# An S5 scan gated by an MLP, on one core: a bias through a broadcast load, B turned by DMA, C loaded late, a warm-up burst and a searched order

## The chip, the cores and the metric

The kernel runs on one core of a Trainium2 chip. A core has five engines that run side by side, each through its own list of instructions in order: TensorE (PE, matrix products into psum), VectorE (DVE), ScalarE (ACT, functions by table), GpSimd (POOL) and SyncE (SP), which here only issues DMAs. They wait for each other through semaphores. Tensors come from HBM into SBUF (128 partitions) by DMA; psum has eight banks. The metric is the device time of one execution in microseconds; of several runs the median is taken.

## The reference

The input x has 2048 rows of D = 448. It is normalised (`xn`), and two branches work on it: a complex diagonal recurrence with P = 448 states (branch A), and an MLP with F = 1792 behind a second LayerNorm (branch B). The result is x + A * silu(B).

```python
def _A_ref(x, ...):                     # x is xn
    Lam, Bmat, Cmat = Lambda_re + 1j*Lambda_im, B_re + 1j*B_im, C_re + 1j*C_im
    Lam_bar = jnp.exp(jnp.exp(log_dt) * Lam)
    B_bar = ((Lam_bar - 1.0) / Lam)[:, None] * Bmat
    Bu = jnp.einsum("bld,pd->blp", x + 0j, B_bar)
    for t in range(L):
        h = Lam_bar[None, :] * h + Bu[:, t, :]
    y = 2.0 * jnp.einsum("blp,dp->bld", hseq, Cmat).real + x * Dskip

def _B_ref(x, w1, b1, w2, b2):
    h = _gelu(jnp.einsum("bsd,df->bsf", _layernorm(x), w1) + b1)
    return jnp.einsum("bsf,fd->bsd", h, w2) + b2

s = _A_ref(xn, ...);  g = _silu(_B_ref(xn, ...));  return x + s * g
```

Weights and x are bf16, as is the output.

## The kernel before

**Tiling.** The rows go in four groups `g` of 512; a group has two blocks `b` of 256 rows, and a block has even and odd rows (`par`). The scan is taken over pairs of rows, so it has 256 steps a group (NK). The matmul stages of a group are:

- `xt`: LayerNorm's results `xn` (branch A) and `xn2` (branch B, its row of ones carries b1) are turned into `xnT` and `xn2T`. For `xn2` of group 0 this is done on PE with `ident` (L390) and copied out by ACT and DVE, for all others by DMA on SP (`dma_start_transpose`, L73).
- `bu(g, i)`: xn times the combined B matrix `BT` into psum bank 4 (L558; 14 matmuls of 256 columns for i = 0, 1, 2, and 7 for i = 3). ACT evacuates it into `u_sb` (L562 to L566), which frees the bank for the next.
- `ssm(g)`: rotation by the tables `WT`, scans on DVE (L583), and rotation back into `h_sb`.
- `mm1(g, j)`: xn2 times w1 (L623, 8 matmuls of 512 columns for each of seven j) into bank pairs 0/1 and 2/3; ACT's gelu (L630) writes `gT[:, g % 2]`.
- `mm2(g, b, par)`: gT times w2 (L637, 14 matmuls) into bank 5 or 6, and one more matmul (L639) that adds b2 by `onesblk` (its first row ones) and `b2blk` (its first row b2). Then ACT's tanh(x/2) (L641), and g = (tanh + 1) * psum on DVE (L642); the halves are folded into other factors.
- `ym(g, b, par)`: h times `CZ` or `CQ`, and the skip through `M0` or `Do`, into bank 7 (L651 to L659); DVE multiplies by g (L663), adds x (L664) and SP stores.

**Preparation.** `parameters` brings the four vectors onto partitions by nine small matmuls (L408 to L412), DVE copies them out (`cp`, L415), and some forty small operations on POOL, with ACT's exp and sin and one reciprocal on DVE (L449), make the coefficients. `tables` makes WT (DVE L479 to L489, ACT L485 to L491). `lb(m)` makes the B matrix that takes two steps at once (`combine`, seven pairs on DVE), and `bt_pe(m)` turns it: seven PE transposes (L520) into bank 6 or 7, one evacuation by DVE (L526) or ACT (L524). C is loaded in twelve pieces into `Cn`, which lies in the half of gT that groups 1 and 3 use (keys GA), over a zero fill by POOL (L284); `ct_dma` turns it with four DMAs into `Cr`, and `cq` combines it into CQ and CZ, fourteen pairs of an ACT scale (L501) and a DVE multiply-add (L504). `m0` multiplies B by CQ (L547, L549).

**What sets the order.** No order is written out by hand. Each operation is a Task with an engine, a planned duration `dur` and latency `lat`, keys that it reads and writes, and a priority. `order()` simulates a list schedule: of all ready tasks it takes the one with the earliest possible start, and at equal starts the lowest `prio`. `emit()` writes the instructions in that order, engine by engine, with the waits that the keys ask for. So a change of a duration or a priority in the code moves instructions everywhere. Each DMA is a task of the engine that issues it and has its own semaphore. Priorities come from the stage: P gives ln -9, bu -8, mm1 0, mm2 5, ym 6, and 10 more for each group; group 0 and the preparation have values of about -100 to -57.

w2 is loaded by two DMAs of POOL, everything else by SP but for the four vectors (ACT).

Of the kernel before, what the change touches and what calls it, by code (L numbers as in the profile page):

```python
# [15 lines left out]
class Task:
# [5 lines left out]
                 "deps", "succ", "start", "end", "name")  # L22

    def __init__(self, eng, ins, reads, writes, dur, lat, prio, sem, nbytes, name):
# [4 lines left out]
        self.start = self.end = None  # L29


class Plan:
# [25 lines left out]
    def add(self, eng, ins, reads=(), writes=(), dur=0.2, lat=0.1, prio=0.0, sem=None, nbytes=0, name=""):  # L58
        if callable(ins):
            ins = [ins]  # L60
        t = Task(eng, ins, reads, writes, dur, lat, prio, sem or eng, nbytes, name)
# [4 lines left out]
    def dma(self, eng, out_ap, in_ap, reads=(), writes=(), prio=0.0, nbytes=0, transpose=False, name="dma"):
# [105 lines left out]
def bass_recurrent_scan__ssm_conv_s5__mixer_channel_mlp__prompt_kernel(  # L172
# [15 lines left out]
    PK = 3  # L188

    kb = Plan(nc)  # L190
    with ExitStack() as es:
# [70 lines left out]
        with nc.Block():  # L262
# [21 lines left out]
            pool(lambda e: e.memset(Cn, 0.0), [], ["Cnp"], 2.0, S0 + 1)  # L284
# [475 lines left out]
```

## Time and profile before

| | us |
|---|---|
| median of three runs | 178.13 |
| lowest and highest of them | 178.11, 179.58 |
| the profiled execution, its own time | 177.91 |
| its span, first to last instruction | 175.9 |

The page of the profile gives, for one execution, the busy time of each engine, the same in 40 slices of 4.4 us, the DMA queues, the chain of work that ended last, and groups of instructions by line with their mean length in ns and the idle time ahead of them. PE's matmuls are pipelined and their ends are modelled: a group's mean length holds the way through the array, and the spacing of matmuls in a stream is read from the chain, where a run of matmuls stands with its length. PEld is the loading of PE's weights, which overlaps the matmuls. An engine's idle time matters only where the chain passes through it.

| part | busy us | of the span |
|---|---|---|
| PE | 157.7 | 90% |
| DVE | 116.2 | 66% |
| ACT | 91.0 | 52% |
| POOL | 35.7 | 20% |

### The profile page before, as it was taken

The numbers are of one execution on the slowest core, as the hardware profiler recorded it, in microseconds if no ns is written. First come the engines' busy times: TensorE is split into PE (matmuls) and PEld (weight loads), VectorE is DVE, ScalarE is ACT, GpSimd is POOL, SyncE is SP. The second block draws the span as 40 slices with busy tenths as digits, with TensorE's granted clock in tenths as the row PEclk, the third lists the DMA queues.
The fourth block names the chain that finished last, engine by engine and source line by source line (L and its number), as shares of the span: only waits on it lengthen the run. The fifth ranks groups of instructions, "written<-read, shape, count | busy, mean of one in ns | idle before, by whom it ended". The sixth has DMA issues, their size and how long they took to land.

```text
span 175.9 us, 2656 instructions
## 1 busy us (share of the span) xinstructions
PE 157.7 (90%) x942; PEld 88.1 (50%) x942; DVE 116.2 (66%) x262; ACT 91.0 (52%) x137; POOL 35.7 (20%) x98
## 2 busy tenths in 40 slices
PE   0149999789989999999999999999999999999971
PEld 0143445666656544545566654656555454455430
DVE  4798997669998997998751499611798722013342
ACT  3047659897879874757182244972326424411200
POOL 8979993000013500320000002120000000000000
PEclk9999999999999999999999999999999999999999
DMA  5999999619300000013953402100000101000011
GB/s 131 332 287 286 310 266 151 123 25 131 72 2 0 4 0 0 0 52 86 130 117 68 104 4 52 52 0 0 4 0 0 52 0 52 4 0 0 0 52 54
DMA packets 25272, 13.21 MB, mean 75 GB/s; under 512 B 19878, under 2 KB 24907, under 8 KB 25260
## 3 DMA queue, kind: packets, MB, share of 16 engines
q1 hardware_dynamic: 24836, 11.45, 30.1%
q0 software_dynamic: 416, 1.61, 2.9%
q8 instruction: 7, 0.11, 0.2%
q14 instruction: 5, 0.04, 0.1%
q10 hardware_dynamic: 8, 0.00, 0.0%
HBM read 6.89 MB, written 1.84 MB: 50 GB/s over the span
## 4 chain that ended last, share of the span: by engine, by line
PE 81%; ACT 8%; POOL 4%; DVE 3%; issue 1%; ACTq 0%; POOLq 0%
PE psum L623 27%; PE psum L637 23%; PE psum L651 12%; PE psum L558 10%; PE psum L655 3%; PE psum L547 2%; POOL gT L284 2%; PE psum L639 2%; DVE t L663 1%; PE psum L390 1%; ACT gT L630 1%; ACT BT L524 1%; PE psum L659 1%; ACT L630 1%; ACT L641 1%
## 5 line engine op out<-in xcount | busy, mean ns | idle before, releaser
L623 PE MATMUL psum<-xn2T,w_sb 128*128 128x512 bf16 x224 | 51.8, 386 | 1.0 <-DVE xn2T L396 1.0
L637 PE MATMUL psum<-w_sb,gT 128*128 128x448 bf16 x224 | 45.0, 352 | 0.8 <-ACT BT L524 0.5
L630 ACT ACTIVATE gT<-psum 128x1024 bf16<-128x1024 f32 x28 | 28.6, 1022 | 25.0 <-PE psum L623 24.8
L623 PEld LDWEIGHTS psum<-xn2T,w_sb 128*128 128x128 bf16 x224 | 21.9, 99 | 26.4 <-issue 1.9
L637 PEld LDWEIGHTS psum<-w_sb,gT 128*128 128x128 bf16 x224 | 21.7, 98 | 20.1 <-issue 0.7
L642 DVE SCALAR_TENSOR_TENSOR g_sb<-th,psum 128x448 bf16<-128x448 f32 x16 | 9.9, 617 | 30.0 <-ACT th L641 30.0
L558 PE MATMUL psum<-xnT,BT 128*128 128x256 bf16 x196 | 24.0, 273 | 1.3 <-ACT u_sb L562 1.3
L558 PEld LDWEIGHTS psum<-xnT,BT 128*128 128x128 bf16 x196 | 18.8, 98 | 5.8 <-PE psum L549 1.1
L641 ACT ACTIVATE th<-psum 128x448 f32<-128x448 f32 x16 | 8.6, 541 | 23.2 <-PE psum L639 23.1
L663 DVE TENSOR_TENSOR t<-psum,g_sb 128x448 bf16<-128x448 f32 x16 | 9.9, 622 | 11.9 <-PE psum L659 6.5
L597 POOL TENSOR_TENSOR cwk<-s_f,ang 128x3 f32<-128x3 f32 x3 | 1.6, 526 | 64.1 <-DVE s_f L583 64.1
L583 DVE TENSOR_TENSOR_SCAN s_f<-cw,cur,v_sb 128x256 f32<-128x256 f32 x21 | 14.5, 736 | 0.0
L651 PE MATMUL psum<-CZ,h_sb 128*128 128x448 bf16 x56 | 11.9, 353 | 0.7 <-DVE t L663 0.7
L651 PE MATMUL psum<-CQ,h_sb 128*128 128x448 bf16 x56 | 11.9, 353 | 0.7 <-DVE t L663 0.7
L562 ACT ACTIVATE u_sb<-psum 128x512 bf16<-128x512 f32 x12 | 7.1, 593 | 7.1 <-PE psum L558 7.1
L345 DVE BATCH_NORM_STATS2 lnst<-x_all 128x6 f32<-128x448 bf16 x16 | 9.6, 616 | 0.9 <-DMA x_all<-in_A_x_dram 0.9
L501 ACT ACTIVATE tmp<-Cr,cw 128x448 f32<-128x448 bf16 x14 | 9.2, 665 | 1.3 <-DVE CQ L504 1.2
L377 DVE TENSOR_SCALAR xn_sb<-x_all,lnw 128x448 bf16<-128x448 bf16 x24 | 8.7, 404 | 1.7 <-DMA xnT<-xn_sb 1.6
L651 PEld LDWEIGHTS psum<-CQ,h_sb 128*128 128x128 bf16 x56 | 5.4, 98 | 6.1 <-DVE t L663 1.2
L651 PEld LDWEIGHTS psum<-CZ,h_sb 128*128 128x128 bf16 x56 | 5.4, 98 | 5.9 <-DVE t L663 0.9
L587 ACT ACTIVATE s_b<-s_f 128x1536 bf16<-128x1536 f32 x4 | 5.9, 1478 | 2.9 <-DVE s_f L583 2.9
L655 PE MATMUL psum<-M,xnT 128*128 128x448 bf16 x32 | 7.4, 353 | 0.0
(130 smaller groups left out, 183.1 us busy)
## 6 DMA issues: line engine op xcount, KB each, us to landing
w_sb<-in_B_w_dram POOLq DMA_DIRECT2D x2, 784.0 KB, 9.4
out_dram<-o_sb SPq DMA_DIRECT2D x7, 224.0 KB, 1.9
w_sb<-in_B_w_dram SPq DMA_DIRECT2D x2, 672.0 KB, 6.5
x_all<-in_A_x_dram SPq DMA_DIRECT2D x3, 448.0 KB, 6.5
x_all<-in_A_x_dram SPq DMA_DIRECT2D x2, 224.0 KB, 2.6
Bn<-in_A_B_re_dram SPq DMA_DIRECT2D x1, 336.0 KB, 8.5
Bn<-in_A_B_im_dram SPq DMA_DIRECT2D x1, 336.0 KB, 7.7
gT<-in_A_C_re_dram SPq DMA_DIRECT2D x1, 288.0 KB, 7.3
```

The costliest lines, as they stand in the source:

```text
L345: dve([lambda e, b=b, par=par, q=q: e.bn_stats(lnst[:, q, :], x_all[:, 2 * g + b, par, :])], [f"x{2 * g + b}"], [f"st{q}"], 0.6, prio)
L501: act(lambda e: e.activation(tmp[:, k, :], b, ACT.Copy, scale=cb), rd, [f"tmp{k}"], 0.66, prio)
L558: fns = [lambda e, r=r, m=m, d=d: e.matmul(psum[:, 4, r * NK:(r + 1) * NK], BT[:, m, d, :], xnT[:, gx, d, :], start=(d == 0), stop=(d == 6 ...
L583: dve(lambda e, i=i, ri=ri, init=init: e.tensor_tensor_scan(s_f[:, i, ri, :], col(R2, i).to_broadcast([128, NK]), v_sb[:, i, ri, :], init, ...
L623: fns = [lambda e, k=k, d=d: e.matmul(psum[:, b0 + k, :], w1_sb[:, d, (2 * j + k) * 128:(2 * j + k + 1) * 128], rhs[:, d, :, :], start=(d ...
L630: act(lambda e: e.activation(gT[:, gb, 2 * j:2 * j + 2, :], psum[:, b0:b0 + 2, :], ACT.Gelu_apprx_tanh), [f"ps{b0}", f"ps{b0 + 1}"] + (WK ...
L637: fns = [lambda e, fi=fi: e.matmul(psum[:, bk, 0:D], gT[:, gb, fi, q * 128:(q + 1) * 128], w2_sb[:, fi, :], start=(fi == 0), stop=False) f ...
L641: act(lambda e: e.activation(th[:, fb, :], psum[:, bk, 0:D], ACT.Tanh, scale=0.5), [f"ps{bk}"] + (WK + WKP if g == 0 else []), [f"th{fb}"] ...
L642: dve(lambda e: e.scalar_tensor_tensor(out=g_sb[:, gs, :], in0=th[:, fb, :], scalar=1.0, in1=psum[:, bk, 0:D], op0=ALU.add, op1=ALU.mult), ...
L651: fns = [lambda e, k=k: e.matmul(psum[:, 7, 0:D], h_sb[:, hb, k, k0:k0 + 128], cm[:, k, :], start=(k == 0), stop=False) for k in range(7)]
L655: fns += [lambda e, d=d: e.matmul(psum[:, 7, 0:D], xnT[:, gx, d, xs], M0[:, d, :], start=False, stop=(d == 3)) for d in range(4)]
L663: dve(lambda e: e.tensor_tensor(t3[:, fb, :], psum[:, 7, 0:D], g_sb[:, gs, :], ALU.mult), ["ps7", f"g{gs}"], [f"t3{fb}"], 0.62, prio - 75)
```

## The change

1. **b2.** `onesblk`, `b2blk` and their fills go, and so does the sixteenth matmul of each mm2. b2 is loaded by one DMA into all 128 partitions (`b2bc`, each partition reads the same 896 B). DVE adds it: `o2` = psum + b2bc, in F32 in SBUF. tanh and g read o2, so the bank of mm2 is free after the add.
2. **B.** `bt_pe` goes. `bt(m)` is one DMA transpose of a whole tile on SP, 128 x 896, seven of them, each behind its `lb(m)`.
3. **C.** Cn lies in four blocks of 112 rows rather than 128, so nothing has to be filled with zeros (POOL's fill goes). It comes in five loads rather than twelve, with priority -40, where the loads ahead of it have the fixed ones below; the columns of Cr are renumbered.
4. **Loads.** Loads of x (first two blocks), w1, b1, B, w2, b2 and blocks 2 and 3 of x have priorities near -1e6 (PINNED = -1e5), which set them in the order of the code; w2 moves from POOL to SP.
5. **Warm-up.** 40 matmuls of `ident` with itself into bank 3 are put first on PE: 28, and 12 that read `cp`, at that place in the code before anything has written it.
6. **LayerNorm.** The ten steps of `ln_scale` are one task (`chain=True`) that nothing is put between.
7. **POOL and DVE.** De and Do, eight scalings of `ident`, move from POOL to DVE.
8. **Order.** Of the tasks of the engine whose task could start first, all that could start within 0.13 us (SLACK) compete, and the lowest priority wins. `search` tries six mixes of the priorities with the length of the path behind each task, then 2500 random changes, and keeps what makes the planned total smallest; pinned tasks are left alone. Some planned durations are new.
9. **Memory.** `o_sb` is now a view of `tmp`.

The core of the diff:

```diff
+PINNED = -1e5
+SLACK = 0.13
...
-        dur = nbytes / 105e3 if transpose else 0.45
+        if transpose:
+            dur = 1.4
...
+            first = min(ready, key=lambda t: (starts[t], t.prio, t.idx))
+            limit = starts[first] + SLACK
+            t = min((t for t in ready if t.eng == first.eng and starts[t] <= limit), key=lambda t: (t.prio, t.idx))
...
+    def search(self, rounds, seed=1):
+        tail = {}
+        for t in reversed(self.tasks):
+            tail[t] = t.dur + max([tail[s] + (t.lat if s.eng != t.eng else 0.03) for s in t.succ], default=0)
...
+        for alpha in (0.0, 0.1, 0.3, 1.0, 3.0, 1000.0):
+            trial([p - alpha * tail[t] if p > PINNED else p for t, p in zip(self.tasks, given)])
...
+        o_sb = tmp.bitcast(BF)
+        b2bc = SB("b2bc", [128, D])
+        o2 = SB("o2", [128, 2, D], F32)
...
-            pool(lambda e: e.memset(Cn, 0.0), [], ["Cnp"], 2.0, S0 + 1)
...
             for q in range(2):
-                ld("pool", w2_sb[:, q * 7:q * 7 + 7, :],
+                ld("sp", w2_sb[:, q * 7:q * 7 + 7, :],
...
+            ld("sp", b2bc[:], dram_ap(B_b2, 0, [[0, 128], [1, D]]), ["b2bc"], 114688, S1 + 7)
+            ldx(2, 2, S1 + 7)
...
+                    ld("sp", Cn[0:112, :, o:o + n], dram_ap(cm, a, [[D, 112], [112 * D, 4], [1, n]]), [f"Cn{o}"], 448 * n * 2, -40, dur=1.2)
...
-            def bt_pe(m, bank, how, prio):
-                pe([lambda e, d=d: e.transpose(psh[:, bank, d * 128:(d + 1) * 128], Bn[:, m, d * 128:(d + 1) * 128],
-                                               ident[:, :]) for d in range(7)], rd, [f"ps{bank}"], 0.5, prio)
...
+            def bt(m, prio):
+                rd = [f"Bn{m // 3}"] if m < 6 else ["Bn60", "Bn61"]
+                kb.dma("sp", BT[:, m, :, :], Bn[:, m, :], reads=rd + [f"LB{m}"], writes=[f"BT{m}"], prio=prio, nbytes=229376, transpose=True)
...
-                fns.append(lambda e: e.matmul(psum[:, bk, 0:D], onesblk[:, :], b2blk[:, :], start=False, stop=True))
...
+                dve(lambda e: e.tensor_tensor(o2[:, fb, :], psum[:, bk, 0:D], b2bc[:], ALU.add), [f"ps{bk}", "b2bc"], [f"oo{fb}"], 0.62, prio - 76)
+                act(lambda e: e.activation(th[:, fb, :], o2[:, fb, :], ACT.Tanh, scale=0.5), [f"oo{fb}"] + (WK + WKP if g == 0 else []), [f"th{fb}"], 0.58, prio - 75)
...
+            for k, (n, rd) in enumerate(((28, []), (12, ["cp"]))):
+                pe([lambda e: e.matmul(psum[:, 3, 0:128], ident[:, :], ident[:, :], start=True, stop=True) for _ in range(n)],
+                   ["ident"] + rd, ["ps3"], n * (0.115, 0.06)[k], 2 * PINNED)
...
-            kb.emit()
+            kb.emit(2500)
```

How the order moves at three places. **First, PE behind mm1 of group 0**, before (L623 is mm1, L520 the transposes of B, L637 and L639 mm2, L558 bu):

```order
L623 MATMUL psum<-xn2T,w_sb 128x512 x56
L520 MATMUL psum<-ident,Bn 128x128 x14
L637 MATMUL psum<-w_sb,gT 128x448 x14
L639 MATMUL psum<-b2blk,onesblk 128x448
L520 MATMUL psum<-ident,Bn 128x128 x14
L558 MATMUL psum<-xnT,BT 128x256 x14
L520 MATMUL psum<-ident,Bn 128x128 x14
L558 MATMUL psum<-xnT,BT 128x256 x14
```

and now (L659 is mm1, L594 bu, L673 mm2):

```order
L659 MATMUL psum<-xn2T,w_sb 128x512 x56
L594 MATMUL psum<-xnT,BT 128x256 x14
L673 MATMUL psum<-w_sb,gT 128x448 x14
L594 MATMUL psum<-xnT,BT 128x256 x14
L673 MATMUL psum<-w_sb,gT 128x448 x14
L594 MATMUL psum<-xnT,BT 128x256 x14
L673 MATMUL psum<-w_sb,gT 128x448 x14
L594 MATMUL psum<-xnT,BT 128x256 x7
L659 MATMUL psum<-xn2T,w_sb 128x512 x8
L594 MATMUL psum<-xnT,BT 128x256 x14
L659 MATMUL psum<-xn2T,w_sb 128x512 x8
L594 MATMUL psum<-xnT,BT 128x256 x14
```

Behind mm1 came transposes and mm2, with bu third; bu is now the first work behind it, and needs xnT and two tiles of BT there. The queue of SP that brings them, before, from the last loads of C on:

```order
L74 DMA gT<-in_A_C_im_dram 64x64
L74 DMA b2blk<-in_B_b_dram 1x448
L74 DMA x_all<-in_A_x_dram 128x2x896 x2
L73 DMA_TRANSPOSE xnT<-xn_sb 128x7x128 x2
L73 DMA_TRANSPOSE Cr<-gT 128x8x128 x3
L73 DMA_TRANSPOSE Cr<-gT 128x8x64
L73 DMA_TRANSPOSE xn2T<-xn_sb 128x8x128 x2
L73 DMA_TRANSPOSE xnT<-xn_sb 128x7x128 x2
```

and now, from w2 on:

```order
L82 DMA w_sb<-in_B_w_dram 128x7x448 x2
L82 DMA b2bc<-in_B_b_dram 128x448
L82 DMA x_all<-in_A_x_dram 128x2x896
L82 DMA gT<-in_A_C_re_dram 112x4x64
L82 DMA gT<-in_A_C_re_dram 112x4x448
L81 DMA_TRANSPOSE xnT<-xn_sb 128x7x128
L81 DMA_TRANSPOSE BT<-Bn 128x7x128 x2
L81 DMA_TRANSPOSE xnT<-xn_sb 128x7x128
L81 DMA_TRANSPOSE BT<-Bn 128x7x128 x3
L82 DMA gT<-in_A_C_im_dram 112x4x384
L81 DMA_TRANSPOSE BT<-Bn 128x7x128 x2
L82 DMA gT<-in_A_C_im_dram 112x4x64 x2
```

The seven BT stand among the loads, the first two between the xnT of group 0; behind these rows come two loads of x, xn2T and xnT of group 1, and then the four Cr, which before stood ahead of xn2T.

**Second, ACT where gelu of group 1 begins** (the first gelu that writes over C). Before, with the waits (s_d37 to s_d40 are the four Cr; L641 is tanh, L562 to L566 the evacuation of bu, L630 gelu, L501 the scale in cq):

```order
L501 ACTIVATE tmp<-Cr,cw 128x448 [waits s_d39,s_d38,s_d37,s_pool,s_d40]
L562 ACTIVATE u_sb<-psum 128x512 [waits s_pe]
L501 ACTIVATE tmp<-Cr,cw 128x448
L501 ACTIVATE tmp<-Cr,cw 128x448 [waits s_dve,s_act]
L641 ACTIVATE th<-psum 128x448 [waits s_pe]
```

and now (L677 is tanh, L598 to L602 the evacuation of bu, L666 gelu, L544 the scale):

```order
L677 ACTIVATE th<-o 128x448 [waits s_dve,s_act]
L598 ACTIVATE u_sb<-psum 128x512 [waits s_pe]
L666 ACT_TABLE_LOAD [waits s_d39,s_d38,s_d37]
L666 ACTIVATE gT<-psum 128x1024 [waits s_d40]
L598 ACTIVATE u_sb<-psum 128x512 [waits s_act,s_pe]
L666 ACTIVATE gT<-psum 128x1024
L544 ACTIVATE tmp<-Cr,cw 128x448 [waits s_pool]
```

The wait for Cr stood at a scale behind the third BT evacuation; it now stands at gelu's table load, with the evacuation of bu(1,1) queued behind it.

**Third, the end of PE.** Before, from the last mm2 on (L651 to L659 are ym):

```order
L637 MATMUL psum<-w_sb,gT 128x448 x14
L639 MATMUL psum<-b2blk,onesblk 128x448
L651 MATMUL psum<-CQ,h_sb 128x448 x7
L658 MATMUL psum<-Do,xnT 128x64
L659 MATMUL psum<-Do,xnT 128x128 x3
L651 MATMUL psum<-CZ,h_sb 128x448 x7
L655 MATMUL psum<-M,xnT 128x448 x4
L651 MATMUL psum<-CQ,h_sb 128x448 x7
L658 MATMUL psum<-Do,xnT 128x64
L659 MATMUL psum<-Do,xnT 128x128 x3
```

and now (L687 to L695 are ym):

```order
L673 MATMUL psum<-w_sb,gT 128x448 x14
L687 MATMUL psum<-CQ,h_sb 128x448 x7
L694 MATMUL psum<-Do,xnT 128x64
L695 MATMUL psum<-Do,xnT 128x128 x3
L673 MATMUL psum<-w_sb,gT 128x448 x14
L687 MATMUL psum<-CZ,h_sb 128x448 x7
L691 MATMUL psum<-M,xnT 128x448 x4
L687 MATMUL psum<-CQ,h_sb 128x448 x7
L694 MATMUL psum<-Do,xnT 128x64
L695 MATMUL psum<-Do,xnT 128x128 x3
```

Three ym stood behind the last mm2; two do now.

227 lines of the change are left out of this document (119 added, 108 removed).

## The prediction

> **What bounds the kernel now.** I read the page first: busy shares, the slices, DMA.
>
> ```profile
> PE 157.7 (90%) x942; PEld 88.1 (50%) x942; DVE 116.2 (66%) x262; ACT 91.0 (52%) x137; POOL 35.7 (20%) x98
> PE   0149999789989999999999999999999999999971
> DMA  5999999619300000013953402100000101000011
> GB/s 131 332 287 286 310 266 151 123 25 131 72 2 0 4 0 0 0 52 86 130 117 68 104 4 52 52 0 0 4 0 0 52 0 52 4 0 0 0 52 54
> ```
>
> A slice is 4.4 us. PE is full from the third slice to the end, but for slices 7 to 9; DMA is full in the first seven slices only. So the time is a start without PE, the PE stream, and an end behind PE. The chain of waits (start us, length us, what) gives the pieces and the pace of each kind of PE work; the waits of PE follow it (total, times, longest).
>
> ```profile
> 1.10 0.27 POOL ident L266
> ...
> 2.19 3.51 POOL gT L284
> ...
> 8.60 0.18 DVE cw L449
> ...
> 10.13 1.90 PE psum L390 x16
> ...
> 12.05 0.70 DVE xn2T L396
> ...
> 13.00 13.54 PE psum L623 x56
> ...
> 28.41 1.28 ACT L485
> ...
> 36.32 0.54 ACT th L641
> ...
> 40.47 0.19 PE psum L639
> 40.66 1.53 PE psum L558 x14
> 42.18 2.65 PE psum L637 x14
> ...
> 45.02 0.78 PE psum L558 x7
> ...
> 60.78 1.73 PE psum L623 x8
> ...
> 166.89 0.64 DVE t L663
> ...
> 169.87 0.64 DVE t L663
> ```
>
> ```profile
> PE psum L408 <- DMA vrows<-in_A_Dskip_dram: 4.9, 1, 4.9
> ...
> PE psum L558 <- ACT u_sb L562: 1.3, 2, 0.8
> PE psum L637 <- ACT BT L524: 0.5, 1, 0.5
> PE psum L520 <- DVE BT L526: 0.4, 1, 0.4
> PE psum L637 <- ACT gT L630: 0.3, 1, 0.3
> ```
>
> The reader sees: PE starts its stream at 13.00, waits 2.5 us in all behind that, and twice more, 0.64 us and some each, at the very end, where ym has one psum bank and DVE must free it. Everything else is PE work. A change gains what it takes out of the PE stream, out of the start, or out of the end, less the new waits it puts into the stream.
>
> **The change part by part.** I write mm1, mm2, bu, ym as the code does; mm2(0,1) is of group 0.
>
> *b2.* Sixteen matmuls of L639 leave PE.
>
> ```profile
> L639 PE MATMUL psum<-b2blk,onesblk 128*128 128x448 bf16 x16 | 5.6, 352 | 0.0
> L642 DVE SCALAR_TENSOR_TENSOR g_sb<-th,psum 128x448 bf16<-128x448 f32 x16 | 9.9, 617 | 30.0 <-ACT th L641 30.0
> ```
>
> The 352 ns hold the drain; the chain's 0.19 us is what one costs in a stream: 16 x 0.19 = 3.0 us off. DVE gets sixteen adds of the same shape from psum, 16 x 0.62 = 9.9 us more; tanh now waits for the add. Between stages DVE has room; its price is below.
>
> *B's transposes.* Forty-nine PE matmuls and seven evacuations go, seven DMAs on SP come.
>
> ```profile
> 26.36 0.94 PE L520 MATMUL psum<-ident,Bn 128*128 128x128 bf16 x14
> ```
>
> 0.94 / 14 = 0.067 us, x 49 = 3.3 us off PE. The waits for BT's evacuations (0.5 + 0.4) go with them: 0.9 off.
>
> *Start.* One row of DVE's timeline first (start, length, and behind it the wait that it ended):
>
> ```profile
> 8.60 0.18 DVE L449 RECIPROCAL cw<-cw 128x4 f32<-128x4 f32 x1 [0.73 <-POOL cw L436]
> ```
>
> The POOL fill of gT (3.51 us) leaves, and De and Do move from POOL to DVE. Before, the fill made the parameter chain on POOL late, the reciprocal at 8.60 waited for it, and LayerNorm queued behind that on DVE. Now the reciprocal stands behind two applies. But 40 warm-up matmuls stand ahead of the parameter matmuls: they need `ident` (1.37) and, at 1.90 / 16 = 0.12 us for the first 28 and half of it for the rest, run until about 5.4 us, 0.5 behind the 4.9 at which the parameter matmuls could start. So `cp` comes 0.5 later, and DVE's aggregates, now behind it, with it. The LayerNorm chain saves 0.73 + 0.18 at the reciprocal, pays that 0.5, and 0.2 for the reciprocal among the applies: transposes at about 10.0. At L520's pace above they take 1.1, the copy 0.7, the hand-overs 0.2: mm1 starts at 12.0, 1.0 off.
>
> *Clock.* The granted-clock row says 1.0 throughout, but matmuls of L623 (count, busy, mean ns) read as two speeds, in 13 to 15 us and in 16 to 26 us:
>
> ```profile
> L623 PE MATMUL psum<-xn2T,w_sb 128*128 128x512 bf16 x5 | 2.3, 622 | 1.0 <-DVE xn2T L396 1.0
> ...
> L623 PE MATMUL psum<-xn2T,w_sb 128*128 128x512 bf16 x48 | 10.5, 379 | 0.0
> ```
>
> At the later pace (1.73 / 8 = 0.216) the 56 would take 12.1, not 13.54: 1.4 off if the warm-up holds. mm1(0) then ends at 12.0 + 12.1 = 24.1, against 26.5.
>
> *End.* The order now puts one ym between the last two mm2, so one wait of DVE's 0.64 us with its hand-over (0.7) goes; the other and the last t, o and store stay.
>
> *Loads and queue of SP.* w2 moves from POOL to SP, ahead of the transposes; C comes in five loads, not twelve, mostly behind B's transposes. First what transposes cost here: issue on SP in ns (min/median/max), landing us, and two stretches of DMA (the last two columns: share, GB/s), the first with four transposes alone, the second inside the run of C's.
>
> ```profile
> L73 SPq DMA_TRANSPOSE xnT<-xn_sb x8: 1222/1544/2271, 21.5 to 105.6; - x8
> L73 SPq DMA_TRANSPOSE Cr<-gT x4: 1309/1344/2468, 25.9 to 31.2; - x4
> ...
> Cr<-gT SPq DMA_TRANSPOSE x4, 4.0
> ...
> 38.00:46.00 8.00, 8.00 (x53) 4.99 (x51) 8.00 (x18) 6.02 (x12) 0.00 (x0) 1.00 0.84 125
> 30.00:32.00 2.00, 2.00 (x25) 1.66 (x24) 0.25 (x3) 2.00 (x5) 0.00 (x0) 1.00 1.25 271
> ```
>
> Upper bound of one: 8 x 0.84 / 4 = 1.67 us of all DMA engines. Lower: 128 x 896 x 2 B = 229 KB at 271 GB/s = 0.85. With a queue standing behind each other, as at 30 us, I take 1.15, nearer the lower. Ahead of them stand, by the arrays' sizes, x 0.92, w1 1.61, B 0.92, w2 1.61, b2 0.11 and C 0.46 MB: 5.6 MB. The GB/s row moves 4.56 MB in four slices (17.6 us) and the rest at 310: done at 21.0. bu(0,0) needs two xnT and two BT: 21.0 + 4 x 1.15 + 0.4 (landing, an allowance) = 26.0, while PE is free at 24.1: **a new wait of 1.9 us** (0.7 to 4.0). It swallows most of what start and clock gain. The next BT follow at 1.15 each under bu and mm2, which take 1.53 + 2.65 per pair: hidden; at 1.67 nearly so.
>
> [...]
>
> *C, late.* gelu of group 1 writes where C lies, so on ACT it waits for all four Cr, and the evacuation of bu(1,1) is queued behind it; bu(1,2) on PE waits for that. When are Cr there? They stand on SP behind the xnT of group 1, whose last apply came 3.9 us behind the first tanh before:
>
> ```profile
> 40.40 0.39 DVE L377 TENSOR_SCALAR xn_sb<-x_all,lnw 128x448 bf16<-128x448 bf16 x1
> ...
> L630 ACT ACTIVATE gT<-psum 128x1024 bf16<-128x1024 f32 x28 | 28.6, 1022 | 25.0 <-PE psum L623 24.8
> ...
> L562 ACT ACTIVATE u_sb<-psum 128x512 bf16<-128x512 f32 x12 | 7.1, 593 | 7.1 <-PE psum L558 7.1
> ```
>
> Now the last gelu of group 0 ends at 25.2; table load to first tanh took 36.86 - 28.41 = 8.45: 33.6; applies 37.5; xnT's issue 1.54, three Cr issues at 1.34, landing 4.0: 47.1. Then a table load of 1.28, gelu 1.02, evacuation 0.59: 50.0. PE comes there at 26.0 + 5 x 1.53 + 0.78 + 4 x 2.65 + 2 x 1.73 = 48.5: **a new wait of 1.5** (0 to 6.8, the latter with 1.67 for each of the 17 transposes and 4.7 us for the loads between: 54.5 + 2.9 - 50.6).
>
> *DVE in the middle.* Busy us of PE, PEld, DVE, ACT:
>
> ```profile
> 40.00:60.00 20.00, 19.22 (x131) 12.43 (x130) 18.81 (x37) 16.47 (x29) 4.00 (x10) 1.00 0.28 41
> 60.00:80.00 20.00, 20.00 (x110) 10.04 (x108) 17.60 (x36) 13.37 (x21) 3.23 (x12) 1.00 0.03 12
> ```
>
> DVE has 3.6 us free in 40, and eight adds, 4.9 us, belong to groups 0 and 1. The order delays the first ym behind four mm2, which gives DVE time. Between 0 and 4.9 I take **1.9**, a little above 4.9 - 3.6, since a queue in order never fills. From 80 us on PE's work is long and DVE's add is hidden beside it.
>
> *Sum*, against the profiled execution: span 175.9, its own time 177.91 (2.0 around it; the median of three runs, 178.13, is 0.2 above). 175.9 - 3.0 - 3.3 - 0.9 - 1.0 - 1.4 - 0.7 = 165.6. The other old waits (1.3 + 0.3) belong to the old order: 164.0. New ones 1.9 + 1.5 + 1.9 = 5.3: 169.3, and 2.0 around it: **171.3 us**.
>
> **The rivals.**
>
> *Transposes starve PE (slower).* If one costs c, the two DMA waits are (21.4 + 4c - 24.1) + (26.1 + 17c + 2.9 - 21.4 - 4c - 22.5) = 17c - 17.6. With DVE's 1.9 the time is 150.3 + 17c: slower by 1% (179.9) from c = 1.74 on. For it: SP's slowest two, 2.27 and 2.47, were issued while loads still queued, as now; at 1.8 the time is 180.9. Against it: the stretch at 30 us runs at half of that.
>
> *The warm-up is lost.* Between the warm-up's end at 5.4 and the first transposes at 10.0 PE idles 4.6 us; the 1.90 us of transposes before mm1 did not bring the clock up either. Then mm1 starts at 12.9 and takes 13.5: its end, 26.4, is 0.4 behind B's landing: 171.7; were B at its early bound, it would cost 1.6 more than the forecast there. [...]
>
> *DVE becomes the bound between 40 and 80 us.* All 4.9 us appear: 174.3.
>
> *All new waits hidden but the least one* (0.7 at B): 166.7. For it: the planner places loads by time; against it: the 5.6 MB ahead.
>
> *The change doesn't do what it says*: excluded for PE's work; the matmuls are gone from the order.
>
> **How the numbers follow.** Forecast 0.50 (169 to 174), warm-up lost 0.20, DVE 0.10, all hidden 0.12, starved 0.08. The time is the forecast's, 171.3. The range reaches to 167.0, near the hidden case, and to 176.5, above DVE's case and with part of the starving one (c = 1.5: 175.8); outside lie half of the hidden and nearly all of the starved case. A measurement of this kernel can tell about 1%: faster is below 176.3, slower above 179.9. Faster 0.83, within 1% 0.10, slower 0.07.
>
> **What would show it.** L520 and L639 gone from PE, PE busy down by 6 to 8 us; the first mm1 at 11.7 to 12.3, its 56 in 12.1 us; PE's longest early wait at bu, released by a transpose, 1 to 4 us, at 24 to 28 us; a second near 48 us released by ACT; one wait, not two, at the end. I am wrong if PE's waits sum to over 8 us, or if DVE has no idle time from 45 to 80 us and PE waits there for it.

## The result, and the profile after

| | before | after |
|---|---|---|
| median of four runs each, same chip, us | 178.69 (178.11 to 179.58) | 172.37 (171.53 to 173.39) |
| ratio, 95% interval | 1 | 0.9645 (0.957 to 0.972) |
| the profiled execution: time, span, us | 177.91, 175.9 | 172.01, 170.3 |

The change makes the kernel 6.3 us faster, within the range that was given. The page of after, in the order of the lines shown of before:

```profile
PE 157.2 (92%) x917; PEld 87.4 (51%) x917; DVE 127.4 (75%) x282; ACT 88.9 (52%) x134; POOL 23.7 (14%) x84
...
PE   6369999979998999999999999999999999999981
...
PEclk9955899999999999999999999999999999999999
```

PE is busy as long as before (157.7), though 65 matmuls of the old stream are gone: the warm-up adds 4.1 us of busy time, and PEclk, which read 9 throughout before, now reads 5 in slices 3 and 4, where mm1 of group 0 starts. Slices are 4.26 us. PE's timeline (start, length, what, and in brackets the wait ahead and what ended it), the rows with a wait:

```profile
1.42 4.07 PE L717 MATMUL psum<-ident 128*128 128x128 bf16 x40 [1.42 <-POOL ident L320]
...
9.38 1.89 PE L433 MATMUL psum<-ident,xn_sb 128*128 128x128 bf16 x16 [3.44 <-DVE xn_sb L420]
12.10 15.20 PE L659 MATMUL psum<-xn2T,w_sb 128*128 128x512 bf16 x56 [0.83 <-ACT ang L473]
27.63 1.69 PE L594 MATMUL psum<-xnT,BT 128*128 128x256 bf16 x14 [0.33 <-DMA xnT<-xn_sb]
...
37.46 1.70 PE L594 MATMUL psum<-xnT,BT 128*128 128x256 bf16 x14 [1.23 <-ACT u_sb L598]
...
52.41 1.69 PE L594 MATMUL psum<-xnT,BT 128*128 128x256 bf16 x14 [0.53 <-ACT u_sb L598]
...
64.21 1.49 PE L583 MATMUL psum<-CQ,Bn 128*128 128x448 bf16 x7 [0.71 <-issue]
```

From 64.2 us on there is one wait more, 0.8 us for DVE's t at the end. So PE's waits inside the stream sum to 2.8 us (0.33 + 1.23 + 0.53 + 0.71), and mm1 of group 0 takes 15.2 us in place of the 12.1 forecast. Why it does is read from stretches of 3.41 us (length, PE busy with its matmuls, granted clock):

```profile
1.04:4.46 3.42, 3.04 (x28) 1.00 0.65 177
4.46:7.87 3.41, 1.42 (x23) 1.00 0.98 285
7.87:11.28 3.41, 1.89 (x16) 0.50 1.10 263
11.28:14.70 3.42, 2.60 (x7) 0.50 1.12 283
14.70:18.11 3.41, 3.41 (x10) 0.50 1.10 339
18.11:21.52 3.41, 3.41 (x17) 1.00 1.17 285
```

The clock goes up at 4.46 us, behind the first warm-up matmuls (the row reads 1.00 ahead of it too, but the matmuls there run at 0.11 us each, behind it at 0.06). In the next 3.41 us PE is busy for 1.42, since the parameter matmuls end at 5.95 and the transposes start at 9.38; the clock falls to half and stays there for three such stretches, until 18.11. The burst is spent before the work it was for. The changes lie 3.41 and 10.24 us apart. The waits at bu stand behind ACT (the 0.71 at m0 names no releaser here; the repeated run below names DVE's CQ there, 0.66). On ACT, with the wait that each row shows:

```profile
33.82 1.15 ACT L534 ACTIVATE WT<-s_f,sgn 128x1024 bf16<-128x1024 f32 x1 [1.29 <-DVE s_f L532]
35.05 1.28 ACT L677 ACT_TABLE_LOAD   x1
...
36.82 0.58 ACT L598 ACTIVATE u_sb<-psum 128x512 bf16<-128x512 f32 x1
...
49.47 1.28 ACT L666 ACT_TABLE_LOAD   x1 [2.84 <-DMA Cr<-gT]
```

The evacuation of bu(0,1) at 36.82 stands behind the W tables and a table load: 1.23 us at bu(0,2). The gelu that overwrites C waits for Cr until 49.47: 0.53 at bu(1,2).

### The profile page after: what moved, and what is told of

The parts are those of the page before. It is cut to its first block, busy times and chain, and to the rows that moved or that the text cites. A ratio compares the mean times of both kernels' runs of the same rounds, so it can differ in the third digit from the quotient of the medians.

```text
span 170.3 us, 2604 instructions
## 1 busy us (share of the span) xinstructions
PE 157.2 (92%) x917; PEld 87.4 (51%) x917; DVE 127.4 (75%) x282; ACT 88.9 (52%) x134; POOL 23.7 (14%) x84
## 4 chain that ended last, share of the span: by engine, by line
PE 78%; DVE 6%; ACT 6%; issue 3%; DMA 3%; SPq 2%; POOL 0%; ACTq 0%; POOLq 0%
PE psum L659 28%; PE psum L673 19%; PE psum L687 13%; PE psum L594 8%; PE psum L691 4%; PE psum L583 3%; DMA Cr<-gT 3%; PE psum L717 2%; SPq L81 2%; DVE xn_sb L420 1%; PE psum L695 1%; ACT L677 1%; ACT L529 1%; DVE t L699 1%; DVE s_f L532 1%
## 5 line engine op out<-in xcount | busy, mean ns | idle before, releaser
L659 PE MATMUL psum<-xn2T,w_sb 128*128 128x512 bf16 x224 | 53.9, 395 | 0.8 <-ACT ang L473 0.8
L673 PE MATMUL psum<-w_sb,gT 128*128 128x448 bf16 x224 | 44.7, 352 | 0.0
L666 ACT ACTIVATE gT<-psum 128x1024 bf16<-128x1024 f32 x28 | 28.7, 1024 | 27.2 <-PE psum L659 26.7
L659 PEld LDWEIGHTS psum<-xn2T,w_sb 128*128 128x128 bf16 x224 | 22.4, 101 | 26.9 <-issue 3.9
L673 PEld LDWEIGHTS psum<-w_sb,gT 128*128 128x128 bf16 x224 | 21.6, 98 | 18.7 <-issue 0.2
L594 PE MATMUL psum<-xnT,BT 128*128 128x256 bf16 x196 | 24.0, 272 | 2.1 <-ACT u_sb L598 1.8
L594 PEld LDWEIGHTS psum<-xnT,BT 128*128 128x128 bf16 x196 | 18.8, 98 | 8.1 <-ACT u_sb L598 1.7
L677 ACT ACTIVATE th<-o 128x448 f32<-128x448 f32 x16 | 9.2, 574 | 21.5 <-DVE o L676 21.5
L676 DVE TENSOR_TENSOR o<-psum,b2bc 128x448 f32<-128x448 f32 x16 | 9.9, 622 | 6.3 <-PE psum L673 6.2
L687 PE MATMUL psum<-CQ,h_sb 128*128 128x448 bf16 x56 | 11.9, 352 | 0.8 <-DVE t L699 0.8
L678 DVE SCALAR_TENSOR_TENSOR g_sb<-th,o 128x448 bf16<-128x448 f32 x16 | 9.9, 619 | 3.3 <-ACT th L677 3.2
L687 PE MATMUL psum<-CZ,h_sb 128*128 128x448 bf16 x56 | 11.9, 352 | 0.0
L598 ACT ACTIVATE u_sb<-psum 128x512 bf16<-128x512 f32 x12 | 7.1, 592 | 7.2 <-PE psum L594 7.1
L633 POOL TENSOR_TENSOR cwk<-s_f,ang 128x3 f32<-128x3 f32 x3 | 0.6, 195 | 68.8 <-DVE s_f L619 68.8
L544 ACT ACTIVATE tmp<-Cr,cw 128x448 f32<-128x448 bf16 x14 | 9.0, 663 | 0.1
L612 DVE TENSOR_TENSOR pb<-u_sb,WT 128x1536 bf16<-128x1536 bf16 x4 | 3.8, 953 | 6.5 <-ACT u_sb L598 6.5
L687 PEld LDWEIGHTS psum<-CQ,h_sb 128*128 128x128 bf16 x56 | 5.4, 98 | 6.3 <-PE psum L691 1.2
L687 PEld LDWEIGHTS psum<-CZ,h_sb 128*128 128x128 bf16 x56 | 5.5, 98 | 5.2
```

The costliest lines, as they stand in the source:

```text
L594: fns = [lambda e, r=r, m=m, d=d: e.matmul(psum[:, 4, r * NK:(r + 1) * NK], BT[:, m, d, :], xnT[:, gx, d, :], start=(d == 0), stop=(d == 6 ...
L659: fns = [lambda e, k=k, d=d: e.matmul(psum[:, b0 + k, :], w1_sb[:, d, (2 * j + k) * 128:(2 * j + k + 1) * 128], rhs[:, d, :, :], start=(d ...
L666: act(lambda e: e.activation(gT[:, gb, 2 * j:2 * j + 2, :], psum[:, b0:b0 + 2, :], ACT.Gelu_apprx_tanh), [f"ps{b0}", f"ps{b0 + 1}"] + (WK ...
L673: fns = [lambda e, fi=fi: e.matmul(psum[:, bk, 0:D], gT[:, gb, fi, q * 128:(q + 1) * 128], w2_sb[:, fi, :], start=(fi == 0), stop=(fi == N ...
L676: dve(lambda e: e.tensor_tensor(o2[:, fb, :], psum[:, bk, 0:D], b2bc[:], ALU.add), [f"ps{bk}", "b2bc"], [f"oo{fb}"], 0.62, prio - 76)
L677: act(lambda e: e.activation(th[:, fb, :], o2[:, fb, :], ACT.Tanh, scale=0.5), [f"oo{fb}"] + (WK + WKP if g == 0 else []), [f"th{fb}"], 0. ...
```

## The experiments

The order comes from a search whose outcome changes with any task. So that one edit moves nothing else, the order of the changed kernel was frozen: its task numbers stand as a constant, and each engine's queue is read from it. Lines of frozen kernels lie 37 higher (45 with b2 on PE, 44 with B on PE), those of DMAs 29 (30 with B on PE). The runs lie on several chips, each with the kernel before measured beside it on the same chip (medians 178.3 to 178.8 us). So runs are compared by their ratio to it, where 0.01 is 1.8 us.

```diff
-        if rounds:
-            self.search(rounds)
-        order = self.order()
+        byidx = {t.idx: t for t in self.tasks}
+        for i in ORDER:
+            if i in byidx:
+                queues[byidx[i].eng].append(byidx[i])
```

Theory A at the start: what left PE (b2, B's transposes) is the gain; the warm-up gives nothing, as transposes and loads hold PE up to 52 us anyway. Rivals: the clock is what the result lacks against the sum; the search carries the gain; or the new DMA transposes cost what they saved.

**The changed kernel again.**

> The changed kernel once more, as the measure for the three that follow on the same chip. Both theories: a ratio to the kernel before of 0.964 within the earlier interval of 0.957 to 0.972, about 6.4 us faster; first mm1 at 12.1 us, its 56 matmuls in 15.2 us, the granted clock back at half from about 8 to 18 us.

172.87 us, ratio 0.970 (0.967 to 0.973). The profiled execution has mm1 at 12.98 and 14.09 us for its 56: the 40 warm-up matmuls took 4.69 us there, and the clock was at half from 9.9 to 16.7 us, where the first profile has it so from 7.87 to 18.11.

**No burst.**

```diff
-            for k, (n, rd) in enumerate(((28, []), (12, ["cp"]))):
+            for k, (n, rd) in enumerate(((1, []), (1, ["cp"]))):
```

> The order of the changed kernel is frozen, and the 28 and 12 warm-up matmuls are cut to one each (they compute nothing that is used). Theory A, the burst is wasted, since PE idles 3.44 us behind it and the clock falls back at 7.9 us until 18.1: same as the changed kernel or up to 1 us faster; the clock goes up no later than 18 us, mm1's 56 matmuls take 13.0 to 15.2 us, and bu of group 0 still starts at 27.6 us or a little before, held by the transposes of xn and B. Rival, the burst is worth the 1.4 us that was forecast: 1.4 us slower, with mm1 starting late or running longer than 15.2 us.

173.30 us, 0.973 (0.969 to 0.977): not to be told from the changed kernel; the rival's 1.4 us lies at the edge of the intervals. The trace speaks against it, since mm1 neither starts late nor runs longer: it ends at 26.6 us here, at 27.3 and 27.1 in the two profiles of the changed kernel. (The execution profiled is the slowest of the six, 174.79 us; at bu(1,2) it waited 1.96 us and had half clock from 54.74 to 58.15.) On PE:

```profile
3.93 0.22 PE L488 MATMUL psum<-ident,vrows 4*128 4x4 bf16 x3 [1.88 <-DMA vrows<-in_A_Dskip_dram]
...
11.67 14.96 PE L696 MATMUL psum<-xn2T,w_sb 128*128 128x512 bf16 x56 [0.83 <-DVE xn2T L476]
27.06 1.70 PE L631 MATMUL psum<-xnT,BT 128*128 128x256 bf16 x14 [0.43 <-DMA xnT<-xn_sb]
```

Without the burst the parameter matmuls start when their data is there, 3.93 rather than 5.42, and mm1 starts 0.4 us sooner. In these profiles the burst costs a little at the start and saves nothing in mm1.

**A longer burst.**

```diff
-            for k, (n, rd) in enumerate(((28, []), (12, ["cp"]))):
+            for k, (n, rd) in enumerate(((28, []), (46, ["cp"]))):
```

The second group also goes behind the parameter matmuls.

> Frozen order; the second warm-up group is moved behind the parameter matmuls and grows from 12 to 46 matmuls, so that PE is busy from 1.4 us until the transposes at 9.4 us. All theories: the clock stays up, mm1's 56 matmuls take 12.1 to 12.5 us in place of 15.2 and end at about 24.3 us. Theory A, the transposes and loads on the DMA engines set the time as far as bu(1,2) at 52.4 us: PE waits about 3.3 us at bu(0,0), which still starts at 27.3 to 27.6 us, and bu(1,2) starts within 0.5 us of 52.4 because Cr still lands at 49.5 us, so the whole is at most 0.5 us faster. Rival, the clock is what cost the changed kernel its 1.7 us against the forecast: 1.5 to 3 us faster, bu(1,2) at 50 to 51 us.

172.83 us, 0.968 (0.965 to 0.971), the same; but the run didn't test what it was for. DVE's copy of the parameters:

```profile
8.13 0.17 DVE L495 COPY cw<-psum 128x12 f32<-128x12 f32 x1 [2.39 <-PE psum L754]
```

The group names `cp` as read, ahead of its writer, so the writer waits for the group. The transposes started 2.2 us later than in the first profile, PE idled 3.5 us again, and mm1 began at half clock (14.79 us for its 56). All expected the clock to hold: wrong.

**The burst fills the gap.** As above with (22, []), (60, []): no `cp`.

> Frozen order; the warm-up is split into 22 matmuls ahead of the parameter matmuls and 60 behind them, and the second group no longer names the copied parameters among its inputs, so that the copy of the parameters on VectorE (which waited in the long burst until 8.1 us) waits for the parameter matmuls alone. Both theories: transposes of xn2 at 9 to 9.5 us, mm1's 56 matmuls in 12.1 to 12.8 us, ending at 24 to 25 us. Theory A, the DMA engines set the time as far as bu(1,2): PE waits 2 to 3.5 us for the transposes of xn and B at bu(0,0), which still starts at 26.9 to 27.7 us, and the whole is within 1 us of the changed kernel. Rival, the clock is worth what it saves in mm1: 2 to 3 us faster than the changed kernel.

172.80 us, 0.966 (0.959 to 0.973). The clock holds and mm1 takes 12.25 us, but nothing is gained. PE, then the same stretches of its clock:

```profile
12.39 12.25 PE L696 MATMUL psum<-xn2T,w_sb 128*128 128x512 bf16 x56 [0.94 <-ACT ang L510]
28.08 3.15 PE L631 MATMUL psum<-xnT,BT 128*128 128x256 bf16 x14 [3.44 <-DMA xnT<-xn_sb]
31.02 4.07 PE L710 MATMUL psum<-w_sb,gT 128*128 128x448 bf16 x14
```

```profile
23.31:26.72 3.41, 1.33 (x7) 1.00 1.13 192
26.72:30.13 3.41, 2.05 (x10) 0.50 0.95 184
30.13:33.55 3.42, 3.42 (x13) 0.50 0.95 197
```

The transposes land at 28 us, little later than the 27.6 of the changed kernel and than theory A's range. PE waits 3.44 us, and the wait takes the clock down: bu and mm2 behind it take 3.15 and 4.07 us where the changed kernel needs 1.69 and 2.81, 2.7 us more. Theory A holds here, and the wait of 3.44 us costs 6.1 us with the slow clock behind it.

**The queue of SP.** Order only, on SP: b2, x blocks 2 and 3 and the first C loads behind the first four transposes, x blocks 4 to 7 behind Cr.

```diff
 w_sb<-in_B_w_dram x2
-b2bc<-in_B_b_dram, x_all<-in_A_x_dram (2, 3), gT<-in_A_C_re_dram x2
 xnT, BT x2, xnT
+x_all<-in_A_x_dram (2, 3), b2bc<-in_B_b_dram
 BT x2
+gT<-in_A_C_re_dram x2
...
-x_all<-in_A_x_dram (4 to 7) x2
 xn2T x2, xnT x2, Cr x4
+x_all<-in_A_x_dram (4 to 7) x2
```

On DVE the first statistics of group 2, which read x block 4, go behind the gate.

> Frozen order on every engine but SyncE, and the short warm-up: on SyncE's queue the loads of x blocks 2 and 3, b2 and the first half of C go behind the first transposes of xn and B, and the loads of x blocks 4 to 7 (0.92 MB) go behind the four Cr transposes; on VectorE the first statistics of block 4 go behind the gate of mm2, so that they don't wait for them. Both theories: Cr lands 2.5 to 3.5 us earlier, at about 46.5 us. Theory A, the queue and mm1's clock set the time together: bu(1,2) gains only what PE waits at bu today, 0.5 to 1.5 us, and the whole is 0.5 to 1.5 us faster than the changed kernel. Rival, the queue alone sets it: 2.5 us or more faster.

173.77 us, 0.972 (0.966 to 0.978), no gain, against both theories: Cr landed at 50.4 us, not 46.5. On DVE the statistics of group 1 waited 2.83 us for x blocks 2 and 3, and what follows them (W, LayerNorm, xn2T and xnT of group 1, all ahead of Cr on SP) came later. SP itself stood idle for 1.75 us ahead of xn2T, so in this run DVE's chain holds Cr. But the block that DVE waited for had been moved back by the same edit, so the run doesn't show what a shorter queue alone is worth.

**Both.** The filled burst and that queue.

> The filled warm-up and the shorter queue ahead of the transposes together. Theory A, each of the two alone is hidden by the other: bu(0,0) at 24 to 25.5 us, Cr landed at about 46.5 us, bu(1,2) at 49.5 to 50.5 us, and the whole 2 to 3 us faster than the changed kernel, more than the two gains alone added together. Rival, the lead is lost again to VectorE, whose inputs don't come sooner: within 1 us of the better of the two alone.

172.03 us, 0.962 (0.957 to 0.968): the intervals of the changed kernel overlap it, and the 2 to 3 us are not shown. The rival's bound holds: 0.7 us better than the better of the two alone. In the profile bu(0,0) starts at 24.04 with no wait, as theory A had it; Cr lands at 47.2 and bu(1,2) starts at 50.61, both a little later than its figures. Then m0 waits:

```profile
63.26 1.50 PE L620 MATMUL psum<-CQ,Bn 128*128 128x448 bf16 x7 [1.56 <-DVE CQ L584]
```

It is 2.1 us ahead of the repeated run at bu(1,2) and 1.2 at m0: DVE has seven statistics and a LayerNorm scale between its CQ products, and PE waits for the last of these.

**b2 back on PE.**

```diff
-                                                 start=(fi == 0), stop=(fi == NF - 1)) for fi in range(NF)]
+                                                 start=(fi == 0), stop=False) for fi in range(NF)]
+                fns.append(lambda e: e.matmul(psum[:, bk, 0:D], onesblk[:, :], b2blk[:, :], start=False, stop=True))
...
-                dve(lambda e: e.tensor_tensor(o2[:, fb, :], psum[:, bk, 0:D], b2bc[:], ALU.add), [f"ps{bk}", "b2bc"], [f"oo{fb}"], 0.62, prio - 76)
-                act(lambda e: e.activation(th[:, fb, :], o2[:, fb, :], ACT.Tanh, scale=0.5), [f"oo{fb}"]
+                act(lambda e: e.activation(th[:, fb, :], psum[:, bk, 0:D], ACT.Tanh, scale=0.5), [f"ps{bk}"]
```

> Frozen order; b2 goes back to TensorE as a 15th matmul of each mm2, and the 16 additions on VectorE are gone (tanh and the gate read PSUM). Theory, PE sets the time and VectorE has room: 16 x 0.19 = 3.0 us slower than the changed kernel (at least 2.5), PE busy 3 us more. Rival, the additions cost on VectorE most of what they save on TensorE: at most 1 us slower, with shorter waits of PE at bu, m0 and ym; or even faster, since VectorE is busy 9.9 us less.

176.68 us, 0.991 (0.987 to 0.995): 3.8 us slower than the repeated run on the same chip, give or take 0.9 by the intervals. The theory holds, and its price was too low. The gate on DVE and PE's stream of this kernel around 70 us, and DVE's add in the repeated run:

```profile
71.26 0.61 DVE L724 SCALAR_TENSOR_TENSOR g_sb<-th,psum 128x448 bf16<-128x448 f32 x1
```

```profile
68.64 0.35 PE L720 MATMUL psum<-b2blk,onesblk 128*128 128x448 bf16 x1
68.83 1.49 PE L628 MATMUL psum<-CQ,Bn 128*128 128x448 bf16 x7
...
71.97 2.81 PE L718 MATMUL psum<-w_sb,gT 128*128 128x448 bf16 x14 [1.60 <-ACT tmp L589]
```

```profile
68.74 0.62 DVE L676 TENSOR_TENSOR o<-psum,b2bc 128x448 f32<-128x448 f32 x1
```

One b2 matmul takes 68.83 - 68.64 = 0.19 us of PE, as forecast. But psum is now read by tanh and by the gate, and mm2's bank comes free at 71.87 (71.26 + 0.61), where the add freed it at 69.36: PE waits 1.6 us. (The row names ACT's tmp, which mm2 doesn't read; the bank is what it has to wait for.) Moving the bias also copied psum out early. That VectorE's adds cost what they save is out.

**B's transposes back on PE.** Seven transposes to a tile as before the change, put by hand between mm1's groups, evacuated by ACT behind the gelus.

```diff
-                kb.dma("sp", BT[:, m, :, :], Bn[:, m, :], reads=rd + [f"LB{m}"], writes=[f"BT{m}"], prio=prio, nbytes=229376, transpose=True)
+                pe([lambda e, d=d: e.transpose(psh[:, bank, d * 128:(d + 1) * 128], Bn[:, m, d * 128:(d + 1) * 128],
+                                               ident[:, :]) for d in range(7)], rd, [f"ps{bank}"])
+                act(lambda e: e.activation(BT[:, m, :, :], psh[:, bank, 0:896].rearrange("p (d c) -> p d c", d=7), ACT.Copy),
+                    [f"ps{bank}"], [f"BT{m}"])
```

> Frozen order; the seven transposes of B go back from the DMA engines to TensorE (49 more matmuls between the mm1 groups) and are copied out by ScalarE behind the gelus. Theory, the move took 49 x 0.067 = 3.3 us off a full TensorE: 1.5 to 3.5 us slower than the changed kernel, as what the DMA engines gain (Cr about 8 us sooner) only takes away the waits at bu (2 us). Rival, the seven transposes cost the DMA engines as much as they saved on TensorE: within 1 us of the changed kernel, or faster.

174.89 us, 0.979 (0.974 to 0.984): by the ratios 1.6 us slower than the repeated run, 2.5 than the first. On PE fourteen take 0.79 us from start to start, 0.056 each:

```profile
20.10 0.94 PE L602 MATMUL psum<-ident,Bn 128*128 128x128 bf16 x14
20.89 1.89 PE L703 MATMUL psum<-xn2T,w_sb 128*128 128x512 bf16 x8
```

49 x 0.056 = 2.8 us. SP's queue without the seven:

```profile
25.38 1.01 SPq L112 DMA_DIRECT2D x_all<-in_A_x_dram  x2
38.80 2.61 SPq L111 DMA_TRANSPOSE xn2T<-xn_sb  x2
```

SP is idle for 12 us and Cr comes no sooner (51.1 us), so the "8 us sooner" expected of both was wrong. xn2T waits for DVE, and DVE for ACT:

```profile
36.40 1.23 DVE L570 SCALAR_TENSOR_TENSOR s_f<-s_f 128x1024 f32<-128x1024 f32 x1 [7.05 <-ACT WT L566]
```

The W tables on ACT start behind the seven evacuations that this edit put there: their table load is at 32.22 us, at 28.38 in the changed kernel. So the price of 1.6 to 2.5 us holds this delay too, beside the PE time, and the run doesn't show what the DMA transposes cost on SP's queue.

**No search.**

```diff
-            kb.emit(2500)
+            kb.emit(0)
```

> The changed kernel with its written priorities, without the 2500 rounds of search over them: the same instructions in the first list schedule's order. Theory, what the change took off TensorE (b2 and the transposes of B) carries the gain and the search little: within 2 us of the changed kernel, with PE busy 156 to 158 us and its waits no more than 2 us longer. Rival, the searched order carries the gain: 4 us or more slower than the changed kernel, near the kernel before, with new PE waits of 1 us and more at bu, m0 or ym.

180.03 us, 1.009 (1.006 to 1.012): 7.0 us by the ratios slower than the repeated run, and slower than before. The rival is right. (This kernel keeps the pinned tasks, SLACK and the new durations: what it lacks is the 2500 tries, and nothing here prices the others.) PE is busy 157.8 us, as it should be; its waits (total, times, longest), and its busy time from 53 to 81 and 81 to 110 us:

```profile
PE psum L687 <- DVE t L699: 5.2, 6, 1.5
...
PE psum L673 <- ACT gT L666: 2.2, 2, 1.1
```

```profile
53.00:81.00 28.00, 26.11 (x141) 1.00 0.00 1
81.00:110.00 29.00, 24.47 (x157) 1.00 0.42 85
```

The repeated run is busy 27.34 and 29.00 there. Here ym stands back to back on one bank, and DVE has LayerNorm in between: what left PE comes back as PE waiting for DVE and ACT.

**A better queue, by hand.** x blocks 2 and 3 ahead of the transposes again, the scale of group 2 and the statistics of group 3 behind CQ on DVE; filled burst, and the same without burst.

> The filled warm-up, and a queue in which x blocks 2 and 3 keep their place ahead of the first transposes (VectorE waited 2.1 us for them in the run before), with b2 and the first half of C behind the first transposes of xn and B, and x blocks 4 to 7 behind Cr; on VectorE the statistics of group 3 and the scale of group 2 go behind the last CQ product. Theory, each wait left over belongs to a chain of loads, VectorE and ScalarE ahead of bu and m0 that can be shortened: PE's two waits at bu fall from 3.8 to under 2 us and the one at m0 from 1.6 to under 0.8, and the whole is 2 to 4 us faster than the changed kernel. Rival, what is gained there comes back as PE waits at mm1 or ym of groups 1 and 2: within 1 us of the changed kernel.

> The kernel of the run before this one with the warm-up cut to one matmul each. Theory, once the transposes land before mm1 ends, the clock in mm1 counts: mm1's 56 matmuls take 14 to 15 us in place of 12.2, bu(0,0) starts 1.5 to 2.5 us later and the whole is 1 to 2.5 us slower than with the filled warm-up. Rival, the chain of VectorE and ScalarE behind mm1 sets the time there in any case: within 0.7 us of it.

174.49 us, 0.977 (0.975 to 0.980), and without burst 173.13, 0.969 (0.966 to 0.972). Both expectations failed: the first is slower than the changed kernel, and the burst loses 1.4 us. Its PE, and the clock:

```profile
36.28 3.17 PE L631 MATMUL psum<-xnT,BT 128*128 128x256 bf16 x14 [3.08 <-DMA BT<-Bn]
```

```profile
32.51:35.92 3.41, 0.69 (x4) 1.00 1.29 147
35.92:39.33 3.41, 3.05 (x15) 0.50 0.97 185
```

With the burst PE reaches bu(0,2) 3 us ahead of its transposes, waits, and pays in clock again (3.17 for 1.69). Both kernels also wait 2.2 us at the second m0; with the burst the clock falls there once more (PEclk reads 6 in the slice from 69.4 to 73.8 us, and m0 takes 2.73 us), without it it doesn't (9, and 1.49 us), and that is part of the 1.4. The cause of the wait: ACT, which frees its bank, waits for a CZ product that stands behind the statistics moved on DVE. That was a mistake of the hand-made order.

**Five moves.** Filled burst, the queue of "Both", and moves against the waits left there.

> The filled warm-up and the queue of the run with both (x blocks 2 and 3 behind the first transposes), with five moves by hand against the waits that were left there: on VectorE the inputs of the W tables and the last two B products go ahead of the statistics that wait for x blocks 2 and 3; on SyncE the transpose of B tile 5 goes ahead of tile 6 and the first C loads behind them; on ScalarE u(0,1) is copied out ahead of the last W table and u(1,1) ahead of the gelu that waits for Cr; on VectorE the statistics of group 3 go behind the last CQ product. Theory: PE's waits at bu (3.8 us) fall under 1.5 us and the one at m0 (1.6 us) under 0.8, and the whole is 2 to 4 us faster than the changed kernel, at 169 to 171 us. Rival, chains that are not seen yet (transposes of xn of group 1, Cr) take their place: within 1 us of the changed kernel, with a PE wait of 1.5 us or more at bu of group 0 or 1 released by a DMA.

170.39 us, 0.954 (0.950 to 0.957): by the ratios 2.9 us faster than the repeated run of the changed kernel, intervals apart, and the fastest of all. mm1 ends at 23.6 us and PEclk reads 9 in every slice. The theory's total holds; its bound on the waits doesn't. PE's waits at bu (L631) and m0 (L620):

```profile
PE psum L631 <- issue: 1.9, 1, 1.9
...
PE psum L631 <- DMA xnT<-xn_sb: 0.8, 2, 0.6
PE psum L620 <- DVE CQ L584: 0.7, 1, 0.7
...
PE psum L631 <- DMA BT<-Bn: 0.6, 1, 0.6
```

3.3 us at bu, where under 1.5 was expected, but the clock stays up behind them (the longest is 1.9), and 0.7 at m0. From "Both" alone (0.957 to 0.968) the run is not clearly apart: the intervals touch.

## Why the prediction came out right

171.3 us forecast, 172.4 measured, 172.9 in the repeat; direction, range and the main reason hold. But the sum is near by luck: two errors cancel, mm1 3.2 us late and the waits 2.5 us short.

- **b2, 3.0 us** (the fifteenth matmul of each mm2, 16 in all): right in kind, 3.8 measured (2.9 to 4.7). The term left out that the add frees mm2's bank early (1.6 us at one mm2). The two would make 4.6; where the rest went is not followed.
- **B's transposes, 3.3 + 0.9:** 1.6 to 2.5 measured, with the delay of the W tables in it. 0.067 per transpose held the last one's way out; from start to start it is 0.056. Of the evacuation waits 0.23 came back.
- **Start, 1.0:** 12.10 in the profiled run, 12.98 in the other, against 13.00: 0 to 0.9, as the burst ahead of the parameter matmuls runs 4.1 to 4.7 us. That the first agrees with the forecast is luck too: the transposes started at 9.38 rather than 10.0 us, but took 1.89 at half clock for the 1.1 forecast.
- **Clock, 1.4:** the failed step. "1.4 off if the warm-up holds": it didn't, and mm1 took 15.2 us, 1.7 more than before rather than 1.4 less. The rival "the warm-up is lost", given 0.20, is what happened; the clock even came up later (18.1 us) than before the change, where the matmuls changed pace between 15 and 16 us.
- **A new wait of 1.9 at bu(0,0):** B and xnT landed at 27.6, not 26.0, but PE came at 27.3: 0.33. Had the clock held, it would have been 3.4 and 2.7 of slow clock on top, as the filled burst shows. The lost warm-up covered this term: with mm1 3.2 us late there was little left to wait.
- **Cr, 1.5:** landed at 49.5 for 47.1, the wait 0.53. The forecast dated it by the last apply, at 37.5 us, then SP. In the changed kernel the applies end at 39.66 us, SP issues without a pause of more than 0.2 us up to the last Cr, and the last apply's transpose (the second xnT below) is issued at 40.95. So SP's queue holds Cr by up to 1.3 us, a term that the forecast lacks:

```profile
34.31 1.00 SPq L82 DMA_DIRECT2D x_all<-in_A_x_dram  x2
35.36 4.20 SPq L81 DMA_TRANSPOSE xn2T<-xn_sb  x2
39.61 2.64 SPq L81 DMA_TRANSPOSE xnT<-xn_sb  x2
42.44 6.26 SPq L81 DMA_TRANSPOSE Cr<-gT  x4
```

In "The queue of SP" and "Both" SP waits for DVE instead (1.75 and 1.33 us idle): with a shorter queue DVE holds Cr.

- **DVE in the middle, 1.9:** 0.71 at m0 in the searched order. In the unsearched order it is the bound, as the rival said.
- **Not foreseen:** 1.23 at bu(0,2), behind W and a table load on ACT.
- **End:** one wait of 0.8, as forecast.

Span: mm1 ended 3.2 us later than forecast (27.3 for 24.1), the waits were 2.8 rather than 5.3: 0.7 net, of the 1.0 by which the span missed. "PE busy down by 6 to 8 us" did not show on the page; 157.7 - 157.2 + 4.1 for the warm-up + 1.7 of slow mm1 is 6.3.

The two edits of PE, each undone alone, are worth 3.8 and 1.6 to 2.5: 5.4 to 6.3 together, against a gain of 5.4 (the repeated run) to 6.3 (the first). If the prices add, which no run with both undone tested, what else changed nets to nothing. But these prices hold in an order that was searched for the changed kernel; an order searched for the old operations was not tried, nor were C's layout, the move of De and Do, the removed fill, SLACK or the pinned loads undone alone. The step that the forecast took for granted is the search: with the written priorities alone the edits gain nothing. Other signs that the prediction named came out otherwise: the longest early wait for a transpose was 0.33 us, not 1 to 4, and the longest at bu, 1.23, was for ACT.

## What to carry to other kernels

Work taken off the bounding engine was a gain here only in the searched order (172.87 us, against 180.03 without the search): price the edit and the schedule apart, with the order frozen. For a warm-up, look at the gap behind it and at when the inputs of the next work land: here the first burst was lost in 3.44 us without PE work, and the filled one kept mm1 at 12.25 us, but its lead ended in a wait of 3.44 us that cost another 2.7 in slow clock. Moving a bias off a matmul into an add also freed the psum bank early here (1.6 us of PE waiting), which is worth a line in the sum.

## What was not expected of the hardware

- The clock fell also where PE was partly busy. In the profiles named here its changes lie 3.41 us or a multiple of that apart: 3.41 and 10.24 in the changed kernel (4.46, 7.87 and 18.11 us); from a fall to the next rise 6.8 in the repeated run (9.9 to 16.7), the longer burst (12.6 to 19.4) and the filled burst (26.72 to 33.55), and 3.41 in the better queue (35.92 to 39.33) and without a burst (54.74 to 58.15). At full clock it fell behind stretches of 3.41 us with 0.10 (the repeated run), 0.69 (the better queue), 1.33 (the filled burst) and 1.42 us of PE work (the changed kernel); it held behind 2.19 (22.27 to 25.68, the better queue) and 2.48 (9.65 to 13.07, the filled burst). At half clock it stayed behind 1.89 and 2.60 (the changed kernel) and 2.05 (the filled burst), and rose behind 2.62 (the kernel before, 12.21 to 15.62, by the pace of its matmuls: 0.62 us in the mean before 15.4, 0.40 from 15.62 on), 3.05 (the better queue) and 3.41 (the changed kernel). PE's busy time is modelled and the stretches are few, so no threshold is shown.
- A DMA's issue on SP had no fixed length here. In the changed kernel b2's load took 2.48 us and the first xnT 4.17; the second xnT took 1.29:

```profile
11.89 2.48 SPq L82 DMA_DIRECT2D b2bc<-in_B_b_dram  x1
...
16.69 4.17 SPq L81 DMA_TRANSPOSE xnT<-xn_sb  x1
...
24.15 1.29 SPq L81 DMA_TRANSPOSE xnT<-xn_sb  x1
```

In the run "The queue of SP" the same load of b2 took 0.46 us behind the transposes. The long ones stand behind many loads; that these are what held them is not shown by a run of its own.
